# Reading the moving operand of the first MoE product in token order, and storing 128 rows with one transfer

## The chip, the cores and the metric

The kernel runs on one core of a Trainium2 chip. The metric is the device time of one execution in microseconds (us): the median of three runs before the change is 230.69 us (230.67 to 230.79). A core has five engines that run side by side and wait for each other through semaphores: TensorE (PE, matrix products; PEld is its loading of the stationary operand), VectorE (DVE), ScalarE (ACT), GpSimd (POOL) and SyncE (SP). In this kernel SP issues every DMA transfer; sixteen DMA engines carry the data out.

## What is computed

Two layers follow each other. The first is a recurrence over 768 positions for 4 batches and 8 heads of 48 channels, with a state of 48 x 48 per head:

```
cur = einsum('bhd,bhe->bhde', u[None] * kt, vt)
y[:, :, t] = einsum('bhd,bhde->bhe', rt, state + cur)
state = wt[:, :, :, None] * state + einsum('bhd,bhe->bhde', kt, vt)
```

Its output, seen as 3072 tokens of 384 channels, goes through a two-layer network with a squared ReLU:

```
h = x @ w_in          # 3072 x 384 by 384 x 2048
g = maximum(h, 0) ** 2
out = g @ w_out       # 3072 x 2048 by 2048 x 384, float32
```

## The kernel before, in words

The work is cut into 12 steps of 256 tokens (four batches, three steps each; `T` is 256). A step's tokens are taken in pairs: the loads (`load_step`, L87) put pair p, that is tokens 2p and 2p+1, on partition p, so that the two tokens of a pair (the parity j) lie side by side. The recurrence works on two chunks of 64 pairs (index c, the pair inside a chunk is q). Its result `y_sb` has on its 128 partitions first the 64 even tokens of a chunk and then the 64 odd ones, in other words the order (j, q), and the two chunks one behind the other along the free axis.

`y_sb` is then transposed into `xT`, a tile of 128 channels by (2 chunks, 3 channel blocks, 128 token columns) in bfloat16: by TensorE in the first four steps (`yt_`, `xt_`, L359 to L369), by a transposing DMA in the later ones (`dyt_`, L371). Its 128 token columns of a chunk have the order (j, q): 64 even tokens, then 64 odd ones.

The first MoE product, `m1_` (L378 to L388), has 8 calls per step; each makes 2 x 3 matmuls at L386 with a 128 x 128 block of `w_in` as stationary operand and the 256 token columns of `xT` as moving operand. So there are 12 x 8 x 6 = 576 of them. Its results stand in PSUM as 128 features by 256 tokens; `rl_` (L390, on ACT or DVE) scales and clips them, `sq_` (L398) squares them into `gt`. The second product, `m2_` (L405 to L411), takes for each chunk c the 128 token columns of `gt` as stationary operand and 384 columns of `w_out` as moving operand: 12 x 2 x 16 = 384 matmuls, into a PSUM tile of 128 tokens by 384. `os_` (L413) copies that to `o_sb`, and `store` (L417) sends `o_sb` to the output. As the 128 rows of `o_sb` are in the order (j, q), the store's destination is written as two groups of 64 rows, each taking every second row of the output.

The order of the instructions on every engine is written out before the program is built: `make_order` (L557) runs through a plan of operations with a rank and an assumed time each, and the resulting order is fixed (L657). On SP the loads, transposing DMAs and stores share one queue in that fixed order, so a DMA whose condition is not yet met holds back everything behind it. Loads of step s use the buffers of step s - 4.

Of the kernel before, what the change touches and what calls it, by code (L numbers as in the profile page):

```python
# [18 lines left out]
def kernel(  # L19
# [13 lines left out]
    nc = tc.nc  # L33
# [3 lines left out]
    C = 128  # L37
# [134 lines left out]
    tiles = {}  # L172
# [204 lines left out]
    def m1_(s, g):  # L377
        if g == 0:  # L378
            tiles["gt", s] = gt_pool.tile([C, NT, T], BF16, name="gt")
        if g % 2 == 0:  # L380
            tiles["rl", s, g // 2] = relu_pool.tile([C, 4, T], FP16, name="rl")
        ps1 = tiles["m1", s, g] = ps_m1.tile([C, 2, T], FP32, name="m1")
        for j in range(2):
            n = g * 2 + j
            for kk in range(KT):
                nc.tensor.matmul(ps1[:, j, :], wi_sb[:, kk, n * 128:(n + 1) * 128],  # L386
                                 tiles["xT", s][:, :, kk, :],
                                 start=(kk == 0), stop=(kk == KT - 1))  # L388

    def rl_(s, g):  # L390
# [25 lines left out]

    def store(s, c):  # L417
        t0 = s * T + c * C
        nc.sync.dma_start(out=out[t0:t0 + C, :].rearrange("(p j) d -> j p d", j=2),
                          in_=tiles.pop(("o", s, c))[:])  # L420

    def warm_(n):
# [77 lines left out]
    for s in range(NS):  # L500
        at = AHEAD + s * 200
        xt = ("dyt_", s) if by_dma(s) else ("xt_", s)
        for g in range(8):
            deps = [xt] + [("cast", "i", g // 2, j) for j in range(KT)]
            if s >= 3:
                deps.append(("m2_", s - 3, 1, 3))
            op("P", .66, at + g, m1_, (s, g), deps, take=("m1",) if g % 2 else ("m1", "rl"))
            op(dict(A=.60, V=.68), None, at, rl_, (s, g), [("m1_", s, g)], give="m1")
            if g % 2:
                op(dict(A=1.05, V=.75), None, at, sq_, (s, g // 2), [("rl_", s, g - 1), ("rl_", s, g)],  # L510
                   give="rl")
        for c in range(2):
            for q in range(4):
                deps = [("sq_", s, q)]
                deps += [("cast", "o", q, j) for j in range(4)]
                if q:
                    deps.append(("m2_", s, c, q - 1))
                op("P", .65, at + AFTER + c * 4 + q, m2_, (s, c, q), deps,
                   take=() if q else ("m2",))
            op("A", .50, at - 5000, os_, (s, c), [("m2_", s, c, 3)] + on("store", s - 2, c), give="m2")  # L520
            op("S", .36, -1, store, (s, c), [("os_", s, c)], dma=(8, .54, 1.0))
# [170 lines left out]
```

## Time and profile before

| what | value |
|---|---|
| median of the runs | 230.69 us |
| the profiled execution | 231.1 us, of which the span on the core 229.3 us |
| PE busy | 195.4 us (85%), 2637 matmuls |
| DVE, ACT, POOL busy | 133.3, 109.0, 109.9 us |
| first product, L386 | 576 matmuls of 256 columns, 278 ns mean |
| second product, L410 | 384 matmuls of 384 columns, 331 ns mean |
| DMA | 36.23 MB, 158 GB/s on average |
| mean granted TensorE clock | 0.967 |

The span is from the first to the last instruction on the core. A matmul's duration contains the time that the result takes through the array, and successive matmuls overlap in it; so the pace of a stream of matmuls is read from how long a run of them lasts, not from the mean of one. The chain of work that ended last is followed back from the last instruction through whatever released each step, and gives the share of the span for which each kind of work, wait or transfer was the last to finish.

### The profile page before, as it was taken

To read this page: it belongs to the slowest core of one execution; us is meant where nothing else is said; L and a number is where in the kernel's file an instruction comes from. 1 tells how busy PE (TensorE), PEld (TensorE's weight loads), DVE (VectorE), ACT (ScalarE), POOL (GpSimd) and SP (SyncE) were. 2 spreads that over 40 slices of the span, in tenths; PEclk is the share of its full clock that TensorE was granted. 3 is DMA by queue.
4 is the path that set the end of the run, shared out by engine and by line. 5 is a ranking of instruction groups with operands and counts; after the bars stand their busy time and mean duration, and the time that the engine had idled before them with its cause. 6 is when DMAs were issued, how large, how long until landed. Compare 5 with 4: busy or idle time off the path is not lost.

```text
span 229.3 us, 6128 instructions
## 1 busy us (share of the span) xinstructions
PE 195.4 (85%) x2637; PEld 130.3 (57%) x2637; DVE 133.3 (58%) x191; ACT 109.0 (48%) x177; POOL 109.9 (48%) x108
## 2 busy tenths in 40 slices
PE   7779999999989598897599994969498899999840
PEld 2335776667657354565366572747275577777520
DVE  4676897868759337283197754846376546445300
ACT  3418968876742466283573653460561332222200
POOL 6399595499983855931947733563720000000000
PEclk9999999999999979999799999999799999999995
DMA  7999999996697689946969659689948216111111
GB/s 170 236 300 377 262 304 362 223 273 174 176 121 209 164 81 238 150 125 168 204 162 219 152 155 138 172 139 177 118 81 104 51 33 65 38 39 38 37 50 38
DMA packets 80218, 36.23 MB, mean 158 GB/s; under 512 B 73408, under 2 KB 78656, under 8 KB 80192
## 3 DMA queue, kind: packets, MB, share of 16 engines
q1 hardware_dynamic: 80192, 35.86, 72.2%
q8 instruction: 20, 0.33, 0.6%
q14 instruction: 6, 0.05, 0.1%
HBM read 25.36 MB, written 4.72 MB: 131 GB/s over the span
## 4 chain that ended last, share of the span: by engine, by line
DMA 36%; PE 33%; SPq 9%; POOL 7%; ACT 4%; issue 4%; DVE 2%; POOLq 0%
PE m L410 14%; PE m L386 14%; DMA v_raw<-in_v_dram 10%; DMA w_raw<-in_w_dram 8%; SPq L93 6%; DMA w_st<-in_moe_w_in_dram 5%; DMA w_st<-in_moe_w_out_dram 4%; DMA k_raw<-in_k_dram 3%; DMA rkT<-rdec_buf 3%; DMA xT<-y_sb 3%; PE att L315 3%; POOL vq L210 2%; POOL ww L177 2%; POOL r_raw L189 1%; SPq L103 1%
## 5 line engine op out<-in xcount | busy, mean ns | idle before, releaser
L386 PE MATMUL m<-xT,wi_sb 128*128 128x256 bf16 x576 | 79.0, 278 | 4.1 <-ACT rl L393 2.6
L410 PE MATMUL m<-wo_sb,gt 128*128 128x384 bf16 x384 | 77.4, 331 | 5.4 <-ACT o_sb L415 5.0
L386 PEld LDWEIGHTS <-wi_sb 128*128 128x128 bf16 x576 | 55.6, 100 | 20.7 <-issue 5.4
L395 DVE TENSOR_SCALAR rl<-m 128x512 f16<-128x512 f32 x50 | 34.3, 690 | 34.7 <-PE m L386 34.7
L410 PEld LDWEIGHTS <-gt 128*128 128x128 bf16 x384 | 35.9, 98 | 25.9 <-issue 8.3
L393 ACT ACTIVATE rl<-m 128x512 f16<-128x512 f32 x46 | 27.1, 594 | 37.8 <-PE m L386 37.5
L276 DVE TENSOR_TENSOR pmT<-att,mask 128x1024 bf16<-128x1024 f32 x24 | 28.6, 1219 | 9.2 <-PE att L270 8.2
L401 ACT ACTIVATE gt<-rl 128x1024 bf16<-128x1024 f16 x24 | 25.3, 1056 | 1.3 <-DVE rl L395 0.7
L197 POOL TENSOR_TENSOR ku<-k_raw,u_bc 128x768 f32<-128x768 f32 x12 | 22.9, 1910 | 5.1 <-DMA k_raw<-in_k_dram 5.1
L210 POOL TENSOR_TENSOR vq<-v_raw,q 128x768 bf16<-128x768 f32 x12 | 17.9, 1491 | 14.0 <-DMA v_raw<-in_v_dram 4.5
L177 POOL TENSOR_TENSOR ww<-w_raw 128x384 f32<-128x384 f32 x11 | 11.0, 1000 | 25.1 <-DMA w_raw<-in_w_dram 25.1
L202 POOL TENSOR_TENSOR ku<-ku,r_raw 128x768 f32<-128x768 f32 x12 | 21.7, 1810 | 0.7
L185 ACT CAST v_bf<-v_raw 128x768 bf16<-128x768 f32 x12 | 10.0, 831 | 24.9 <-DMA v_raw<-in_v_dram 24.9
L415 ACT ACTIVATE o_sb<-m 128x384 f32<-128x384 f32 x24 | 11.7, 487 | 19.0 <-PE m L410 18.7
L403 DVE TENSOR_TENSOR gt<-rl 128x1024 bf16<-128x1024 f16 x24 | 18.1, 752 | 3.1 <-ACT rl L393 1.6
L425 PE MATMUL m<-warm 128*128 128x512 bf16 x61 | 18.0, 425 | 1.2 <-DVE half_ones L145 1.2
L193 POOL TENSOR_TENSOR k_raw<-k_raw,w_raw 128x384 f32<-128x384 f32 x11 | 11.7, 1062 | 8.6 <-DMA k_raw<-in_k_dram 8.1
L270 PE MATMUL att<-rkT 64*64 64x128 bf16 x384 | 8.9, 222 | 6.5 <-DMA rkT<-rdec_buf 6.4
L206 DVE TENSOR_REDUCE q<-ku 128x16 f32<-128x768 f32 x12 | 11.3, 944 | 5.1 <-POOL ku L202 5.1
L305 POOL TENSOR_TENSOR S<-t_state,a_c 128x192 bf16<-128x192 f32 x20 | 11.4, 571 | 6.0 <-DVE t_state L301 5.8
L301 DVE TENSOR_TENSOR t_state<-S,att 128x192 f32<-128x192 bf16 x16 | 5.6, 351 | 14.7 <-POOL S L305 11.7
L181 ACT ACTIVATE lw_buf<-ww 128x384 bf16<-128x384 f32 x12 | 6.2, 517 | 15.0 <-POOL ww L177 11.8
(64 smaller groups left out, 177.8 us busy)
## 6 DMA issues: line engine op xcount, KB each, us to landing
w_raw<-in_w_dram SPq DMA_DIRECT2D x12, 384.0 KB
r_raw<-in_r_dram SPq DMA_DIRECT2D x12, 384.0 KB
k_raw<-in_k_dram SPq DMA_DIRECT2D x12, 384.0 KB
v_raw<-in_v_dram SPq DMA_DIRECT2D x12, 384.0 KB
out_dram<-o_sb SPq DMA_DIRECT2D x24, 192.0 KB
w_st<-in_moe_w_in_dram SPq DMA_DIRECT2D x4, 768.0 KB
w_st<-in_moe_w_out_dram SPq DMA_DIRECT2D x4, 768.0 KB
rkT<-rdec_buf SPq DMA_TRANSPOSE x16
```

The source lines that it names most:

```text
L177: mul(ww[:], raw["w", s][:, :, 0, :], raw["w", s][:, :, 1, :])
L197: nc.gpsimd.tensor_mul(ku[:], raw["k", s][:, :, 1:3, :], u_bc[:, :, None, :].to_broadcast([C, H, 2, D]))
L202: nc.gpsimd.tensor_mul(ku[:], ku[:], raw["r", s][:, :, 0:2, :])
L210: nc.gpsimd.tensor_mul(vq[:].rearrange("p j h d -> p h j d"), raw["v", s][:], tiles.pop(("q", s))[:, :, :, None].to_broadcast([C, H, 2, D]))
L276: nc.vector.tensor_mul(tiles["pmT", s][:, f].rearrange("p a j t -> p a (j t)"), tiles.pop(("p", s, f))[:].rearrange("p e (a x) -> p (e a) ...
L386: nc.tensor.matmul(ps1[:, j, :], wi_sb[:, kk, n * 128:(n + 1) * 128], tiles["xT", s][:, :, kk, :], start=(kk == 0), stop=(kk == KT - 1))
L393: nc.scalar.activation(rl, m1[:], AF.Relu, scale=RS)
L395: nc.vector.tensor_scalar(out=rl, in0=m1[:], scalar1=RS, scalar2=0.0, op0=ALU.mult, op1=ALU.max)
L401: nc.scalar.activation(gt, rl[:], AF.Square)
L403: nc.vector.tensor_mul(gt, rl[:], rl[:])
L410: nc.tensor.matmul(tiles["m2"][:], gt[:, n, c * C:(c + 1) * C], wo_sb[:, n, :], start=(n == 0), stop=(n == NT - 1))
L425: nc.tensor.matmul(ps[:], warm[:, 0:C], warm[:], start=True, stop=True)
```

## The change

Two places change together. The first product's moving operand is still the same 256 columns of `xT`, but read in token order: for each chunk c and each pair q, first the even token and then the odd one. The innermost step of that reading is 64 elements (128 bytes), and then it goes back by 63. The PSUM tile, `rl`, `gt` and `o_sb` thus have their tokens in the order of the output. The store then names 128 successive rows of the output, instead of two groups of 64 interleaved rows.

```diff
@@ m1_
                 nc.tensor.matmul(ps1[:, j, :], wi_sb[:, kk, n * 128:(n + 1) * 128],
-                                 tiles["xT", s][:, :, kk, :],
+                                 tiles["xT", s][:, :, kk, :].rearrange("p c (j q) -> p c q j", j=2),
                                  start=(kk == 0), stop=(kk == KT - 1))
@@ store
         t0 = s * T + c * C
-        nc.sync.dma_start(out=out[t0:t0 + C, :].rearrange("(p j) d -> j p d", j=2),
+        nc.sync.dma_start(out=out[t0:t0 + C, :],
                           in_=tiles.pop(("o", s, c))[:])
```

The order of instructions is the same on all five engines; on SP the 24 stores have another shape (128 x 384 in place of 2 x 64 x 384), at the same places in the queue.

## Prediction

> **What bounds the kernel now.** I read the page's busy shares first, then the costliest groups, the table of stretches, the chain, and last what the DMA engines do at the end. The table of stretches has the columns start:end, length, busy time of PE, PEld, DVE, ACT and POOL (with instructions), granted clock, DMA share and GB/s.
>
> ```profile
> PE 195.4 (85%) x2637; PEld 130.3 (57%) x2637; DVE 133.3 (58%) x191; ACT 109.0 (48%) x177; POOL 109.9 (48%) x108
> ```
> ```profile
> 23.80:60.00 36.20, 35.41 (x525) 24.85 (x524) 29.59 (x44) 28.67 (x51) 28.26 (x23) 1.00 0.96 257
> 60.00:180.00 120.00, 100.45 (x1509) 67.57 (x1509) 68.52 (x90) 56.72 (x90) 65.15 (x57) 0.96 0.83 153
> 180.00:220.70 40.70, 39.60 (x361) 28.05 (x359) 19.59 (x28) 12.73 (x22) 0.00 (x0) 1.00 0.19 42
> ```
>
> TensorE is the bound from the first MoE matmul (about 24 us) to the last (220 us): it is idle for 0.8 us of the first stretch, 19.6 us of the second and 1.1 us of the third. The second stretch is the only one with slack, and its chain shows what that slack waits for: loads and transposing DMAs that land late.
>
> ```profile
> 96.92 11.01 DMA w_raw<-in_w_dram
> ...
> 127.68 7.59 DMA w_raw<-in_w_dram
> ...
> 143.54 7.51 DMA v_raw<-in_v_dram
> ...
> 153.31 7.91 DMA v_raw<-in_v_dram
> ```
>
> From 180 us on the chain is the two products alone, back to back, in whole runs:
>
> ```profile
> 197.84 1.31 PE m L386 x12
> 199.15 1.30 PE m L410 x8
> ```
>
> These two lines give the pace of a stream: 1.31 us / 12 = 109 ns for 256 columns, and 1.30 / 8 = 163 ns for 384. Both are 0.425 ns per column, so the moving columns set the pace and the weight loads (98 ns) lie beside them. Full clock is granted there.
>
> After the last matmul only the store is left. SP's waits and the stretch 221.3 to 225.0 us, in which nothing but stores moves:
>
> ```profile
> SPq L687 <- DMA out_dram<-o_sb: 7.0, 1, 7.0
> ```
> ```profile
> 221.30:225.00 3.70, 0.00 (x0) 0.00 (x0) 0.00 (x0) 0.00 (x0) 0.00 (x0) 0.91 0.13 49
> ```
>
> A DMA share of 0.13 of 16 engines is two engines. They move 49 GB/s, so one store of 128 x 1536 B = 196.6 KB occupies them for 4.0 us, where 16 engines at the same 24.5 GB/s each would need 0.5 us.
>
> **The change part by part.** *The store.* The 24 stores stay at their places in SP's queue and keep their bytes, 1536 B rows and issue cost (0.52 us median). The slowest dimension of the transfer goes from 2 to 128. I read the two busy engines as following from the two groups, so that 128 rows spread over all 16, as the 128-partition loads do (stretches of 362 and 377 GB/s on the page can't come from two engines at 24.5).
>
> At the end: SP's last store takes 0.5 us to issue and 7.0 more to land, partly behind the store before it. The nearest row for a transfer over 16 engines is the very first load, twice as large: issued at 0.74 us, its reader starts at 4.6 us, so 3.9 us. That saves 3.6 us at least; at the other end a store behind nothing, cut by the full difference of 3.5 us for itself and what is left of its predecessor (240 rows are still to go at 220.7 us, 112 of them the predecessor's, 3.4 us at that pace), saves some 5. I take 4.4, with nothing to hide it: SP's final wait is the end of the program.
>
> In the middle: a load is spread over all engines, so it is only complete when the two that carry a store have come to its rows. On SP a store stands directly ahead of each of the four loads quoted; each could land up to 4.0 - 0.5 = 3.5 us earlier (the first has two stores ahead). That is 14 us at most, and nothing at least, since PE may then wait for transposing DMAs or a POOL result instead (7.0 us of the chain is one xT transpose, next to one of the loads). I take 8 where PE is otherwise unchanged; where the first product grows, this gain is part of the slack that is filled.
>
> *The first product.* 576 matmuls keep 256 columns, weights, PSUM order and neighbours; only the reading of the moving operand changes, so that no two successive elements are neighbours in memory. No row of before reads any operand of PE that way. Lower bound: 109 ns as now; a gain is excluded, because a column per array tick is the pace of both products already. Upper bound: the slowest row with an operand whose order is changed on the way, POOL's vq at 1491 ns for 768 columns = 1.94 ns per column, 497 ns per matmul, +388 x 576 = 223 us. Between them, DVE shows what adjacent 16-bit elements are worth to an engine: L403 (16-bit, 752 ns for 1024 columns) against L193 (32-bit, 557 ns for 384), each less the 59 ns of a one-column memset, is 0.68 against 1.30 ns per column, a factor of 1.9 for elements that come as neighbouring pairs. PE's moving operand is 16-bit too; without neighbours it would fall to one column per two ticks. PE has that pace itself in its first microseconds at half clock: ten warm-up matmuls of 512 columns in 4.44 us, 0.83 to 0.87 ns per column. So I take 2 x 109 = 216 ns, +107 ns x 576 = +61.6 us, on the path wherever PE is the bound. Reads by ACT and DVE of the results are unchanged.
>
> What absorbs of it: PE's idle time between 23.8 and 220.7 us, 21.5 us. In the third stretch 149 of the matmuls find 1.1 us of slack, in the first about 120 find 0.8. The other 307 add 33 us to a stretch with 19.6 idle, most of it DMA waits, which a step longer by 5 us and the lighter engines cover. Some of it stays (the transposes, PSUM waits for o_sb, 5.0 us in all). I take 14, with 5 and 20 as ends. If that cover were gone the cost would be the full 61.6.
>
> [...]
>
> *Sum.* The profiled execution is 231.1 us (span 229.3 and 1.8 around it), 0.4 above the median. 231.1 + 61.6 - 14 - 4.4 = 274.3; against the median 274.
>
> **Rivals.**
>
> *The strided read is free (or under 1.2 x).* Two streams, even and odd, each advance in order, and a small buffer per stream would do; PE then stays at 0.425 ns per column. For it: stationary and moving operands already come at 98 and 109 ns with no interference. Against it: 16-bit operands show the pair effect above. Time: 230.7 - 4.4 - 8 = 218, from 212 (all 14 in the middle) to 226 (nothing there). This is the case on the other side. It decides as long as 576 times the extra time stays under the gains plus the idle time filled: with 12.4 us gained that is 22 ns per matmul, a factor of 1.2; filled idle time moves the point to some 1.25.
>
> *A partial penalty, 1.2 to 1.7 x.* At 1.5: 55 ns x 576 = 31.4, less 14 and 4.4: 244 us. Range 228 to 255.
>
> *A penalty of 3 to 4.6 x.* At a factor of 4: 326 x 576 = 188, less 20 of idle time and 4.4: 394 us; up to 430 at the POOL bound. For it: PE asks for a new element every 0.42 ns, faster than any other engine here reads, so memory may fall short by more than the pair.
>
> *The store's two engines are not due to the two groups.* Then the tail keeps its 7.0 us and the forecast is 4.4 us higher, 278. Against it: loads with 128 partitions reach seven times the rate.
>
> **How the numbers follow.** Free 0.29, partial 0.10, about two times (1.8 to 2.5) 0.41, more 0.20; the store case is within each. The likeliest one gives 274, with 20 or 5 us absorbed 268 to 283, and with a factor of 2.5 (+94 us, 18 and 4.4 off) 303; its own range is 264 to 305. The range over cases must reach down to the free one and leaves out the heavy one: 212 to 310. A measurement of this kernel tells about 0.2% (0.5 us) from no change. Faster 0.29 from the free case with a little of the partial one, slower 0.69, and 0.02 between.
>
> **What would show it.** In the profile after: a run of 12 L386 in the last 40 us takes 2.6 us in place of 1.31 (right), 1.31 (free) or 5 (heavy). L410 stays at 1.30 for 8. PE's idle time between 60 and 180 us falls below 10 us. The last stores move at several hundred GB/s, a DMA share far over 0.13 for half a microsecond each, and SP's final wait falls from 7.0 to 2 to 3.5 us. DVE's and ACT's waits for L386 grow by some 50 us together. The prediction is wrong if L386's pace is not near two ticks per column; the rest of the sum moves it by less than 10 us.

## The result, and the profile after

The changed kernel takes 274.93 us (median of four runs, 274.77 to 275.31) against 230.74 us (230.67 to 231.47): a ratio of 1.191, 95% interval 1.188 to 1.194. It is 44 us slower; the forecast was 274, in a range of 212 to 310. As the experiments show, the two largest terms behind that number, the price of the read and what absorbs of it, were both too small, and their errors cancelled.

The page of the kernel after, its busy times and the two products' groups:

```profile
PE 265.3 (97%) x2631; PEld 128.1 (47%) x2637; DVE 134.2 (49%) x191; ACT 110.5 (40%) x177; POOL 109.0 (40%) x108
...
L386 PE MATMUL m<-xT,wi_sb 128*128 128x256 bf16 x576 | 153.5, 405 | 0.1
...
L410 PE MATMUL m<-wo_sb,gt 128*128 128x384 bf16 x384 | 75.6, 326 | 0.6 <-ACT o_sb L415 0.6
...
out_dram<-o_sb SPq DMA_DIRECT2D x24, 192.0 KB, 2.0
```

A first-product matmul went from 278 ns to 405; the second product did not move. The last line is from the part on DMA issues: a store now lands 2.0 us after its issue. The chain near the end of the kernel after (start, duration, what):

```profile
253.79 2.92 PE m L386 x12
256.70 1.30 PE m L410 x8
```

Twelve matmuls of 256 columns take 2.92 us, 243 ns each, where they took 1.31 us: 0.95 ns per column in place of 0.425. Eight of the second product still take 1.30. The table of stretches of the kernel after, with the same columns as in the prediction:

```profile
60.00:180.00 120.00, 120.00 (x1395) 58.72 (x1388) 63.17 (x80) 56.96 (x88) 64.01 (x57) 1.00 0.67 144
180.00:264.00 84.00, 84.00 (x602) 39.45 (x601) 33.28 (x46) 20.45 (x33) 7.84 (x7) 1.00 0.14 37
```

PE is not idle at all in the stretch where it had 19.6 us of slack, and the granted clock of that stretch went from 0.96 to 1.00. SP's final wait:

```profile
SPq L687 <- DMA out_dram<-o_sb: 1.4, 1, 1.4
```

It fell from 7.0 us to 1.4. So both halves of the change did what the forecast named: the read slowed the first product about twofold, and the store got out of the way. What each is worth by itself is not to be read from these two traces alone.

### The profile page after: what moved, and what is told of

Read it like the earlier page. It is cut to its first block, busy times and chain, and to the rows that moved or that the text cites. A ratio compares the mean times of both kernels' runs of the same rounds, so it can differ in the third digit from the quotient of the medians.

```text
span 273.0 us, 6122 instructions
## 1 busy us (share of the span) xinstructions
PE 265.3 (97%) x2631; PEld 128.1 (47%) x2637; DVE 134.2 (49%) x191; ACT 110.5 (40%) x177; POOL 109.0 (40%) x108
## 4 chain that ended last, share of the span: by engine, by line
PE 90%; DMA 2%; ACT 2%; POOL 1%; DVE 1%; SPq 1%; issue 0%; POOLq 0%; ACTq 0%
PE m L386 52%; PE m L410 24%; PE att L315 6%; PE att L270 2%; DMA k_raw<-in_k_dram 2%; PE att L290 2%; PE m L425 1%; ACT wi_sb L116 1%; POOL ku L197 1%; PE att L219 1%; PE tr L245 1%; POOL ku L202 1%; PE att L220 1%; DVE rdec_buf L234 1%; SPq L121 0%; PE tr L364 0%
## 5 line engine op out<-in xcount | busy, mean ns | idle before, releaser
L386 PE MATMUL m<-xT,wi_sb 128*128 128x256 bf16 x576 | 153.5, 405 | 0.1
L386 PEld LDWEIGHTS <-wi_sb 128*128 128x128 bf16 x576 | 54.5, 98 | 69.4 <-issue 1.0
L410 PE MATMUL m<-wo_sb,gt 128*128 128x384 bf16 x384 | 75.6, 326 | 0.6 <-ACT o_sb L415 0.6
L410 PEld LDWEIGHTS <-gt 128*128 128x128 bf16 x384 | 35.4, 97 | 33.3 <-issue 2.1
L197 POOL TENSOR_TENSOR ku<-k_raw,u_bc 128x768 f32<-128x768 f32 x12 | 22.1, 1841 | 5.0 <-DMA k_raw<-in_k_dram 5.0
L202 POOL TENSOR_TENSOR ku<-ku,r_raw 128x768 f32<-128x768 f32 x12 | 22.6, 1880 | 0.7
L425 PE MATMUL m<-warm 128*128 128x512 bf16 x55 | 16.9, 434 | 1.3 <-DVE half_ones L145 1.2
L234 DVE TENSOR_TENSOR rdec_buf<-r_raw,att 128x768 bf16<-128x768 f32 x12 | 11.4, 950 | 3.4 <-ACT att L227 3.4
L234 DVE TENSOR_TENSOR rdec_buf<-k_raw,att 128x768 bf16<-128x768 f32 x12 | 11.3, 946 | 0.0
L189 POOL TENSOR_TENSOR r_raw<-r_raw,w_raw 128x384 f32<-128x384 f32 x11 | 11.0, 998 | 0.0
L357 ACT CAST y_sb<-att 128x768 bf16<-128x768 f32 x9 | 7.2, 798 | 7.1 <-PE att L315 7.0
```

Source lines behind the costliest of these rows:

```text
L197: nc.gpsimd.tensor_mul(ku[:], raw["k", s][:, :, 1:3, :], u_bc[:, :, None, :].to_broadcast([C, H, 2, D]))
L202: nc.gpsimd.tensor_mul(ku[:], ku[:], raw["r", s][:, :, 0:2, :])
L234: nc.vector.tensor_mul(rdec[:, i, :, :, 0:D], x.rearrange("p h j d -> p j h d"), cs[:, i, 0:DM].rearrange("p (h d) -> p h d", h=H)[:, None ...
L410: nc.tensor.matmul(tiles["m2"][:], gt[:, n, c * C:(c + 1) * C], wo_sb[:, n, :], start=(n == 0), stop=(n == NT - 1))
L425: nc.tensor.matmul(ps[:], warm[:, 0:C], warm[:], start=True, stop=True)
```

## The experiments

### Each half alone

The store alone: before, with

```diff
-        nc.sync.dma_start(out=out[t0:t0 + C, :].rearrange("(p j) d -> j p d", j=2),
+        nc.sync.dma_start(out=out[t0:t0 + C, :],
```

> The columns are read as before (even tokens, then odd ones) and only the store has its new form, so the rows of each output tile land in the wrong order: this is a measurement of the store alone. My theory: the read is the whole loss and the store is a gain of its own, 4 to 6 us at the end (SP's final wait 1.4 us in place of 7.0) plus something in the middle, where loads no longer queue behind a store: 217 to 224 us. Rival: the late loads in the middle have another cause than the store's two engines; then only the end is gained, 225 to 226 us. Second rival: a store over 16 engines disturbs the other transfers and slows the kernel; then 231 us or more.

Measured: 198.87 us (198.63 to 199.33), ratio 0.862 (0.855 to 0.869). This is far below both the theory's 217 to 224 and the rival's 225. The store's new form is worth 32 us by itself. Its stretches:

```profile
23.80:60.00 36.20, 35.29 (x556) 25.01 (x557) 30.55 (x43) 29.29 (x51) 28.69 (x24) 1.00 1.13 279
60.00:150.00 90.00, 90.00 (x1422) 62.85 (x1421) 65.08 (x86) 54.89 (x87) 63.21 (x55) 1.00 0.95 191
150.00:190.00 40.00, 40.00 (x396) 28.70 (x395) 22.67 (x31) 12.46 (x21) 0.00 (x0) 1.00 0.15 46
```

TensorE's idle time is gone here as well, with a first-product matmul at a median of 273 ns as in the kernel before. So slow matmuls were not needed to fill that time: the stores had made it. The waits for loads (engine, waited for, total, times, longest), first before, then with the new store:

```profile
POOL ww L177 <- DMA w_raw<-in_w_dram: 25.1, 7, 7.0
ACT v_bf L185 <- DMA v_raw<-in_v_dram: 24.9, 9, 6.0
PE att L270 <- DMA rkT<-rdec_buf: 6.4, 4, 3.1
```
```profile
POOL ww L177 <- DMA w_raw<-in_w_dram: 3.7, 2, 2.2
ACT v_bf L185 <- DMA v_raw<-in_v_dram: 0.8, 1, 0.8
```

50 us of waits for two inputs shrink to 4.5, and PE's wait for a transposing DMA (`rkT`) is not among the waits on DMA of the new store at all. Transposing DMAs, like loads, occupy most of the sixteen engines: near 191.5 us of the kernel before, one of them beside a store brought the DMA share to 0.9, where stores alone leave 0.13. So they too could be held up by the two engines that carried a store. SP's queue was held up as well: the issues of the 48 loads of the recurrence lasted 87.6 us in all before and 63.8 with the new store, those of the 24 transposing DMAs 53.3 and 37.7. How the gain divides between later landing and later issuing is not shown by these runs.

The read alone: before, with only the `rearrange` in `m1_`.

```diff
-                                 tiles["xT", s][:, :, kk, :],
+                                 tiles["xT", s][:, :, kk, :].rearrange("p c (j q) -> p c q j", j=2),
```

> The columns are read in token order and the store keeps its two groups of 64 rows, so the rows of each output tile land in the wrong order: a measurement of the read alone. My theory: TensorE is never idle once the read is slow, so the store is worth only the end of the program, 5.6 us (SP's final wait 7.0 against 1.4): 280 to 282 us, PE still idle for less than 2 us between 60 and 180 us. Rival: the idle time was filled because the stores got out of the loads' way; with the old stores some 10 us of it come back: 288 to 292 us.

Measured: 280.67 us (280.62 to 280.74), ratio 1.216 (1.208 to 1.223): the theory's number, against the rival's 288 to 292. Its stretch and its final wait:

```profile
60.00:180.00 120.00, 120.00 (x1390) 58.72 (x1387) 63.08 (x80) 56.95 (x88) 64.08 (x57) 1.00 0.72 148
```
```profile
SPq L687 <- DMA out_dram<-o_sb: 7.2, 1, 7.2
```

The old stores cost nothing in the middle once TensorE is slow enough to wait for nobody: from the first MoE matmul to the last, the traces have 245.8 us with either store. Only the end (5.7 us between 280.67 and 274.93) is left of them. The four kernels make a square: from the old store to the new one is worth 32 us with the plain read and 5.7 with the strided one; the strided read costs 50 us with the old store and 76 with the new one.

### Where the store's 32 us lie

New form for the last step's two stores only, and the complement:

```diff
+        rows = out[t0:t0 + C, :]
+        if s < NS - 1:      # the complement: s >= NS - 1
+            rows = rows.rearrange("(p j) d -> j p d", j=2)
+        nc.sync.dma_start(out=rows, in_=tiles.pop(("o", s, c))[:])
```

> The columns are read as before; only the two stores of the last step are one transfer of 128 successive rows, the other 22 keep their two groups (the last tiles' rows land in the wrong order). My theory: the last stores are worth what the two final waits show, 7.0 against 1.4 us, and nothing else: 225 to 226 us. Rival: the gain of the store alone comes from the end of the program; then about 200 us.

> The complement: the 22 stores of the first eleven steps are one transfer of 128 successive rows, the two of the last step keep their two groups (rows of the first tiles land in the wrong order). My theory: the 26 us beyond the end's 5.6 are TensorE's idle time between 60 and 180 us, and come from these: about 199 + 5.6 = 204 to 205 us, and PE idle for less than 2 us in that stretch. Rival: the parts of the gain depend on each other; then the two runs do not add up to the 32 us of the whole.

Measured: 224.50 us (224.20 to 225.35), ratio 0.974 (0.968 to 0.980), with the last two stores alone, against a kernel before at 230.52 in the same comparison; 204.37 us (204.10 to 206.48), ratio 0.889 (0.881 to 0.897), with the other 22. That is 6.0 us at the end and 26.1 in the middle; together 32.1, against 32.6 for the store alone in its own comparison. The rival that they depend on each other falls. The stretch 60 to 180 us of the kernel with only the last stores new, and of its complement:

```profile
60.00:180.00 120.00, 104.51 (x1514) 69.17 (x1503) 69.77 (x90) 56.83 (x90) 64.42 (x56) 0.91 0.81 152
```
```profile
60.00:180.00 120.00, 120.00 (x1758) 84.53 (x1747) 82.55 (x109) 64.79 (x103) 63.43 (x56) 1.00 0.74 155
```

The first keeps 15.5 us of idle TensorE and a mean clock of 0.91; the second has neither and gets through 1758 matmuls in the time of 1514.

### How the loss grows

Token order only in every second call of the first product, with the new store:

```diff
-                                 tiles["xT", s][:, :, kk, :].rearrange("p c (j q) -> p c q j", j=2),
+                                 tiles["xT", s][:, :, kk, :].rearrange("p c (j q) -> p c q j", j=2)
+                                 if g % 2 else tiles["xT", s][:, :, kk, :],
```

> Only every second call of the first product reads in token order, 288 of 576 matmuls; the store has its new form. Half of the features get another token order than the rest, so the output is scrambled: a measurement of how the loss grows. My theory (idle time of TensorE fills first, then every slow matmul counts in full): the slow matmuls add 288 x 134 ns = 38.6 us to TensorE's work; against the changed kernel's 275 that is 236 if TensorE stays busy throughout, and up to 241 if some of the waits come back. Rival (the loss is proportional from the first slow matmul): half way between the new store alone, about 220, and 275: 247 us.

Measured: 235.87 us (235.84 to 235.99), ratio 1.017 (1.013 to 1.022). The number fits "TensorE is busy throughout" (236). But the rival's 247 stood on a wrong value for the kernel with no slow matmuls; with the measured 199 its half way is 237. So this run does not tell the two apart. It shows that with the new store the loss is close to proportional, 37 us for 288 slow matmuls and 76 for 576, as there is no idle time left to fill.

### What a column costs in another order

Eight reading orders in one kernel, told apart by their lines (shortened):

```diff
+                x = tiles["xT", s][:, :, kk, :]
+                if n % 8 == 0:     # L388: x
+                elif n % 8 == 1:   # L390: x.rearrange("p c (a b) -> p c b a", b=2)
+                elif n % 8 == 2:   # L392: the same with b=4
+                elif n % 8 == 3:   # L394: b=8
+                elif n % 8 == 4:   # L396: b=16
+                elif n % 8 == 5:   # L398: x.rearrange("p c (j q) -> p c q j", j=2)
+                elif n % 8 == 6:   # L400: x.rearrange("p c (q e) -> p q c e", e=2)
+                elif n % 8 == 7:   # L402: the same with e=8
```

> The first product's matmuls read their 256 columns in eight different orders, 72 matmuls each, each order on a line of its own: plain; steps of 2, 4, 8 and 16 elements (4, 8, 16, 32 bytes); the changed kernel's order (64 elements on, 63 back); and two orders that alternate between the chunks (384 elements apart) in runs of 2 and of 8 neighbours. The tokens of different features get different orders, so the output is scrambled and only the durations count; a matmul's plain duration is 273 ns and the changed kernel's 404. Theory 1 (elements are fetched as neighbouring pairs): plain and the runs of 2 and 8 stay near 273; every step from 2 on takes 380 to 405, the step of 2 as much as the others. [...]

The groups of that kernel, each with busy time and mean ns of one, and the start of two runs of three in its chain:

```profile
L396 PE MATMUL m<-xT,wi_sb 128*128 128x256 bf16 x72 | 37.0, 634 | 0.0
L394 PE MATMUL m<-xT,wi_sb 128*128 128x256 bf16 x72 | 36.8, 630 | 0.0
L398 PE MATMUL m<-xT,wi_sb 128*128 128x256 bf16 x72 | 21.9, 411 | 0.0
L392 PE MATMUL m<-xT,wi_sb 128*128 128x256 bf16 x72 | 20.2, 399 | 0.0
L400 PE MATMUL m<-xT,wi_sb 128*128 128x256 bf16 x72 | 14.2, 309 | 0.0
L402 PE MATMUL m<-xT,wi_sb 128*128 128x256 bf16 x72 | 12.5, 284 | 0.0
L390 PE MATMUL m<-xT,wi_sb 128*128 128x256 bf16 x72 | 12.1, 275 | 0.0
L388 PE MATMUL m<-xT,wi_sb 128*128 128x256 bf16 x72 | 11.8, 273 | 0.0
```
```profile
24.82 0.68 PE m L392 x3
25.49 1.35 PE m L394 x3
```

Some matmuls of lines 400 and 402 ran at half the granted clock, which raises their means (below, under "Ticks or time"); their medians are 300 and 273 ns, so runs of 8 cost nothing (273 ns plain).

The theory is refuted, and with it the step that my forecast's factor of two rested on: by line 390 a step of two elements, which has no neighbouring pairs, adds only 2 ns (275 against 273). A step of four takes 399 ns, but steps of 8 and 16 take 630 and 634, far more than the theory's 405. The chain gives the paces: three matmuls take 0.68 us with a step of 4 and 1.35 us with a step of 8, that is 227 and 450 ns each, 0.89 and 1.76 ns per column.

From a step of 2 to one of 4 and from 4 to 8 elements (4, 8 and 16 bytes) the time per column about doubles: 0.43, 0.89, 1.76 ns. From 8 to 16 elements (32 bytes) a matmul takes hardly any longer (634 against 630 ns). So the four rows look as if each new piece of 16 bytes, called a line here, cost 1.76 ns, an estimate from these rows alone: a step of 8 takes a new line for every column, 1.76 ns; a step of 4 for every second column, 2 x 0.89 = 1.77 ns; a step of 2 for every fourth, 4 x 0.43 = 1.7 ns, which is just the plain pace. Counted like this, the order of this change also changes line at every column, and costs only 0.95 ns (line 398, three in 0.73 us). It comes back to the line that it left, and a second ladder asks whether that matters. Its orders, on 256 neighbouring elements `flat` of `xT`:

```diff
+                # L389: flat; L392, L395: flat.rearrange("p (a j q) -> p a q j", j=2), q=8 and q=32
+                # L398, L401: flat.rearrange("p (j q) -> p q j"), j=2 and j=4
+                # L404, L407: flat.rearrange("p (j q e) -> p q j e", j=2), e=2 and e=4
+                # L410: flat.rearrange("p (a b) -> p b a", b=8)
```

> A second ladder of reading orders, eight of them on lines of their own, 72 matmuls each, on 256 neighbouring elements of xT (so the products are not the reference's; only durations count; plain is 273 ns). Line 389 plain; 392, 395, 398: two streams read in turn, 8, 32 and 128 elements apart; 401: four streams 64 elements apart; 404 and 407: two streams 128 apart in runs of 2 and 4; 410: one stream with steps of 8 elements. Theory 1 (what was seen: one 16-byte line per 1.76 ns on a stream that never comes back, 630 ns; two lines stay held so that alternating streams cost half): two streams near 405 at any distance, four streams near 630 or more, runs of 2 near 310, runs of 4 near 280, steps of 8 near 630. Theory 2 (the cost depends on which memory bank the next line lies in): the two-stream orders differ strongly among each other with the distance, from 273 to 630.

```profile
L410 PE MATMUL m<-xT,wi_sb 128*128 128x256 bf16 x72 | 36.3, 623 | 0.0
L401 PE MATMUL m<-xT,wi_sb 128*128 128x256 bf16 x72 | 35.0, 604 | 0.0
L395 PE MATMUL m<-xT,wi_sb 128*128 128x256 bf16 x72 | 21.5, 406 | 0.0
L398 PE MATMUL m<-xT,wi_sb 128*128 128x256 bf16 x72 | 21.4, 405 | 0.0
L392 PE MATMUL m<-xT,wi_sb 128*128 128x256 bf16 x72 | 21.4, 405 | 0.0
L404 PE MATMUL m<-xT,wi_sb 128*128 128x256 bf16 x72 | 14.1, 305 | 0.0
L407 PE MATMUL m<-xT,wi_sb 128*128 128x256 bf16 x72 | 12.1, 276 | 0.0
L389 PE MATMUL m<-xT,wi_sb 128*128 128x256 bf16 x72 | 11.9, 274 | 0.1
```

Two streams in turn cost 405 to 406 ns whether they are 8, 32 or 128 elements apart, so theory 2, a cost that differs strongly with the distance, is refuted at these distances. Four streams cost 604, close to the 623 of steps of 8. Runs of 2 add 31 ns to the plain 274, runs of 4 add 2. That fits the first theory's numbers, but not its picture: if two lines were simply held, two streams would need few new lines and should be free. No run shows what is held, and why going back and forth between two streams costs 0.95 ns per column, and not 0.425 or 1.76, stays open.

### Ticks or time

The warm-up matmuls alone read in the changed order:

```diff
-            nc.tensor.matmul(ps[:], warm[:, 0:C], warm[:], start=True, stop=True)
+            nc.tensor.matmul(ps[:], warm[:, 0:C], warm[:].rearrange("p (c j q) -> p c q j", c=4, j=2), start=True, stop=True)
```

> Only the 61 warm-up matmuls of 512 columns, whose results are not used, read in pieces of 128 in the changed order (64 elements on, 63 back); the rest is as before. They run partly at half clock (ten in 4.44 us before) and partly at full clock (five in 1.24 us). Theory 1 (the read needs its ticks at TensorE's clock): 2.28 times as long in both, ten in about 9.9 us at half clock and five in 2.6 us at full clock. Theory 2 (the memory delivers an element every 0.95 ns whatever TensorE's clock): at half clock ten in about 5.0 us, only 0.95 against 0.83 ns per column; at full clock five in 2.6 us. The time of the kernel is 231 to 245 us, as the warm-up lies ahead of the first product on TensorE.

Measured: 239.17 us in one run, with the kernel before at 232.5. Its first TensorE work (start, duration):

```profile
1.19 5.50 PE L425 MATMUL m<-warm 128*128 128x512 bf16 x11 [1.19 <-DVE half_ones L145]
...
6.95 2.58 PE L425 MATMUL m<-warm 128*128 128x512 bf16 x5
9.81 3.06 PE L425 MATMUL m<-warm 128*128 128x512 bf16 x6
```

Between a run of 5 and a run of 6 lies one matmul: 0.48 us for 512 columns, 0.94 ns per column. The eleven in the first 5.50 us also start 0.48 us apart, although plain ones at that point take twice as long as later (in the kernel before they start 0.43 us apart there, and 0.215 later). These are theory 2's numbers. They tell a time from a number of ticks, however, only if the slow start comes from a slower TensorE clock, and the profile's record of the granted clock begins 5.9 us into the kernel before and 5.3 us into this one; ahead of that its column reads 1.00 without a record.

The first ladder settles it. From 36.95 to 40.35 us it was granted a clock of 0.50, and three matmuls in the changed order took 0.73 us there as at full clock (first fence, from its chain). The kernel before was granted 0.50 from 111.7 to 115.1 us, and the twelve plain matmuls that ran there, nearly all within that time, took 2.27 us in place of 1.31 (second fence, from its chain).

```profile
37.58 0.73 PE m L398 x3
...
60.73 0.73 PE m L398 x3
```
```profile
113.26 2.27 PE m L386 x12
```

So theory 2 fits: this order cost 0.95 ns per column at a granted clock of 1.00 and of 0.50 alike, a time per element and not a number of TensorE's ticks, and that this is about twice the plain 0.425 ns is a coincidence of the full clock.

### Versions that keep the gain without the cost

The first version reads runs of 64 neighbours, first the even tokens of both chunks and then the odd ones, so that an output tile holds the tokens of one parity:

```diff
-                                 tiles["xT", s][:, :, kk, :],
+                                 tiles["xT", s][:, :, kk, :].rearrange("p c (j q) -> p j c q", j=2),
...
-        t0 = s * T + c * C
-        nc.sync.dma_start(out=out[t0:t0 + C, :].rearrange("(p j) d -> j p d", j=2),
-                          in_=tiles.pop(("o", s, c))[:])
+        rows = out[s * T:(s + 1) * T, :].rearrange("(p j) d -> j p d", j=2)
+        nc.sync.dma_start(out=rows[c], in_=tiles.pop(("o", s, c))[:])
```

> The columns are read in runs of 64 neighbours: first the even tokens of both chunks, then the odd ones. An output tile then holds the 128 tokens of one parity, and its store is one transfer of 128 rows that takes every second row of the output. All of the computation is there. My theory (hops cost only where they come at every element, and the store's engines follow from its slowest dimension, 128): a run of 12 first-product matmuls stays at 1.31 us, stores land in about 2 us, time within 1 us of the kernel with the new store alone, 217 to 224 us. Rival: leaving the plain order costs in itself, however long the runs; then 12 matmuls take 2.9 us and the time is near 275 us. Second rival: rows with a gap between them keep the store on two engines; then 230 us.

Measured: 199.15 us (198.51 to 200.13), ratio 0.863 (0.857 to 0.869), within 0.3 us of the store alone. From its chain, and its part on DMA issues:

```profile
181.49 1.31 PE m L386 x12
```
```profile
out_dram<-o_sb SPq DMA_DIRECT2D x24, 192.0 KB, 2.8
```

The first product keeps its plain pace, and a store with every second row of the output lands in 2.8 us, just as with successive rows (2.8 as well): the gap between the rows costs nothing. Both rivals fall. Of the kernels here that compute everything, this one has the lowest median; the next version is within the noise of it.

The second version stores the tile with two transfers of 64 rows and leaves the read as it was:

```diff
+        o_sb, rows = tiles.pop(("o", s, c)), out[t0:t0 + C, :].rearrange("(p j) d -> j p d", j=2)
+        for j in range(2):
+            nc.sync.dma_start(out=rows[j], in_=o_sb[j * Q:(j + 1) * Q, :])
```

> The columns are read as before; an output tile is stored by two transfers of 64 rows, one per parity. All of the computation is there. My theory: each transfer's slowest dimension is 64, so both spread over 16 engines; the end and the middle gain as with one transfer, less the 24 extra issues of some 0.4 us on SP, which has waits of its own before most stores: 218 to 226 us. Rival: the extra issues hold back loads and transposing DMAs behind them in SP's queue by 24 x 0.4 = 10 us: 228 to 232 us.

Measured: 199.91 us (199.80 to 201.02), ratio 0.867 (0.861 to 0.873). Splitting the transfer by hand, with the read untouched, gives nearly the whole gain; against the store alone the 24 extra issues on SP cost about 1 us, far from the rival's 10.

## Why the prediction was right, and where it was not

*The bound and the path.* TensorE bound the kernel from 24 to 220 us, as read, apart from the idle time that the stores made, and the slow read lay on that path. The chain after is about 90% PE.

*The price of the read* was mis-sized: +107 ns per matmul was taken, 134 ns measured (243 against 109), so +77 us in place of +61.6. The factor of 2.2 lies inside the stated 1.8 to 2.5, but the step that gave 2, 16-bit elements fetched as neighbouring pairs, was wrong: the step of two elements refutes it (275 ns against 273). The warm-up row was no support either: no clock is on record for it, and at a granted 0.50 the plain pace falls (twelve matmuls in 2.27 us in place of 1.31) while the changed order's does not (three in 0.73 us). What the forecast calls an array tick is the 0.425 ns of a plain column at a granted clock of 1.00.

*What absorbs it* was mis-sized the other way: 14 us, with 20 as the upper end. Between the first and the last MoE matmul the time grew from 196.2 to 245.8 us, by 49.6; against +77 that is 28 us absorbed. TensorE's idle time between these two matmuls went from 20.9 to 0.8 us, which makes 20 of them. The clock makes 5: the kernel before was granted half of it in three pieces of 3.4 us (its mean is 0.91 in each of the stretches 80 to 100, 100 to 120 and 160 to 180 us), the kernel after in none. Where the remaining 2 to 3 us come from is open. The forecast counted idle time but not the clock. Each of the three pieces lies next to a wait of TensorE of 2.1 to 3.7 us; but a wait of 3.1 us that ended at 143.6 us was followed by none, and the first ladder has three such pieces where TensorE hardly waits at all, so these runs do not show that idle time alone lowers the clock.

*The end* came out near: 4.4 us taken, 5.6 measured in the final wait, 5.7 between the two strided kernels.

*The sum* was right by luck: the error of the read, 15 us too little, and that of the absorption, 14 us too little, cancelled. The forecast was +61.6 - 14 - 4.4 = +43.2; the traces give +77 - 28 - 5.6 = +43, where their spans (229.3 and 273.0) differ by 43.7 and the medians by 44.

*The signs named ahead.* L410, the idle time and the last stores came as said (the profile after has 337 GB/s in a slice of 0.6 us near its end). Three had the right direction and another size: twelve of L386 took 2.92 us, not 2.6; SP's final wait fell to 1.4 us, not 2 to 3.5; and the waits of DVE and ACT for L386 grew from 72 to 169 us, by 97 and not by some 50.

*The gain in the middle*, if the read were free, was the worst step: "14 us at most", taken as 8. The runs give 26. With the new store alone the time from the first MoE matmul to the last is 170.1 us in place of 196.2, with 1.5 us of idle time in place of 20.9 and no piece at half clock. The bound counted four loads, each behind a store on SP's queue, and 3.5 us for each (the fourth, at 153.31 us, has a load of `k` between the store and itself). It left out the transposing DMAs, the lower clock, and that SP is held up while it issues. That a late load also delays the next buffer's release, and so the next load, is likely but not shown by itself. Had the read been free, the time would have been 199 us, below the whole stated range of 212 to 310 and outside that rival's 212 to 226; the mechanism was right and its size was not bounded.

*The store's two engines* followed from its two groups: named as a step, and shown by stores of 128 rows landing in 2.0 to 2.8 us by the median, where the two engines at their 49 GB/s would need 4.0 for the bytes of one. That 64 rows do it too is seen in the time alone (199.91 us).

*The rivals:* a free read is refuted by the 243 ns, but would have been met by runs of 4 (276 ns against 274 plain) or a step of 2 (275 against 273). The penalty of four times exists (steps of 8: 450 ns); the order chosen here is just not that one. A partial penalty of 1.2 to 1.7 is excluded by the measured 2.2.

## What to carry to other kernels

Look at a store's slowest dimension: here two groups put it on two of sixteen engines (49 GB/s), and what is spread over many more, loads (up to 377 GB/s) and transposing DMAs (a DMA share of 0.9) alike, came late. A DMA share near 0.13 while only stores moved was the sign. The price is not to be counted on the few transfers behind a store in the queue: compare the idle time of the bounding engine instead, as nearly all of it may come from there, as it did here. When an order has to change, change it in runs (here at least 4 neighbours, 276 ns against 274; 64 in the version that won) and let the transfer's own row step do the fine interleaving (2.8 us to landing here, with the gap between rows and without).

When two edits come together, run each alone: one was worth 32 us, the other cost 76, and the pair looked like a simple loss of 44.

## What the runs showed of the hardware

TensorE's moving operand, 16-bit, cost per column, by how long runs of three to twelve matmuls lasted: 0.425 ns plain; 0.89 ns with steps of 4 elements; 1.76 to 1.80 with steps of 8 or 16; 0.95 when two streams alternate element by element, 8, 32, 64 or 128 elements apart; about 1.7 with four streams. Estimates, from the mean of one matmul less the plain one (273 or 274 ns): 0.43 with steps of 2 elements (275), 0.55 in runs of 2 (305) and 0.43 in runs of 4 (276). The 0.95 ns stayed the same where the granted clock was 0.50 in the first ladder (three in 0.73 us); in the kernel before, plain matmuls ran at about half their pace at that clock (twelve in 2.27 us, nearly all within it, in place of 1.31). Loading the stationary operand beside it stayed at a median of 98 ns with the changed order.
